# Filler products in TensorE's planned gaps among the first chunks, and GpSimd's fills behind its first weight transfers

## The chip, the cores and the metric

The kernel runs on one core of one Trainium2 chip. The metric is the device time of one execution in microseconds (us). Before the change it is 734.04 us, the median of three runs (733.62 to 735.03).

## What is computed

All is float32. A gated linear recurrence runs over 768 steps for 4 batches and 8 heads with 48 features each; its result, 3072 rows of 384 features, goes through an RMS norm and a SwiGLU feed-forward of width 1536.

```
# attention: per batch and head, state S of 48 x 48, complex gate a = a_re + i a_im
mag = sqrt(a_re^2 + a_im^2);  a = a * min(mag, 0.999) / (mag + 1e-6)
for t in range(768):
    S = a_t * S + k_t v_t^T          # complex, row-wise gate
    y_t = q_t . Re(S)
# feed-forward, over 3072 rows x of 384
xn  = x / sqrt(mean(x^2) + 1e-6) * rms_g
out = (silu(xn @ w_gate) * (xn @ w_val)) @ w_out      # 384 -> 1536 -> 384
```

The weights arrive as 64-bit words and are narrowed to float32 on the chip.

## The kernel before, in words

**Chunks, units, groups.** The sequence is cut into chunks of 128 steps: 6 per batch, 24 in all. The gates are worked out per unit (`gates`, line 990): units 0 and 1 are chunk 0 and chunk 1 alone, all others are two chunks. Two chunks make a group, and `feed` (line 1198) runs the feed-forward of a group.

**From gate to product.** For a unit, ScalarE and VectorE work out the size and the angle of the gates and the running products of both; at the end VectorE multiplies q and k with sines and cosines into a tile `rot` (lines 1057 to 1061, two products of 128x768 a chunk, about 0.95 us each). Because a head's features lie on other partitions in `rot` than TensorE needs them, six DMAs on SP's queue carry a chunk's `rot` to the tile `kq` (line 1063). With `kq` there, `attend` (line 1078) makes on TensorE: the scores `bank<-kq` (64 matmul records), masked by two `copy_predicated` into `am`; two sets of transposes `bank<-ident,kq`, copied by ScalarE to `kt`; the result `bank<-am,ve` (and `bank<-kq,state` from chunk 1 on), where `ve` is the chunk of v, loaded by DMA; and the state's increment `bank<-vn,kt`. Then the norm: ScalarE squares into `sq`, TensorE sums it with `ones`, VectorE writes `ssv`, GpSimd takes the power into `rs`, TensorE spreads it (`bank<-ident,rs`), VectorE writes `xT`. When both chunks of a group have their `xT`, the group's feed-forward runs: twelve blocks of 12 records `bank<-xT,wg` and `bank<-xT,wv` (128x256 each), then the products with `wo`.

**Weights.** `narrow` (line 906) loads twelve pieces of the weights through GpSimd's DMA queue: six of 1536 KB (gate and value parts in turns), then six of 768 KB. Three places hold raw words, so the fourth transfer must wait until VectorE has finished the first piece; `fetch` (line 885) also makes it wait for the landing of chunk 0's `kq` (`CLEAR`), and the first for the landing of the first gate load (`begun`). For each piece ScalarE converts the low words, and VectorE shifts, combines and adds: 0.95, 1.76 and 1.76 us for a large piece.

**What sets the order.** Nothing is issued as it is written. `Flow.add` (line 519) records each step with an engine, a cost, its reads and writes; `dates` (530) gives due times backwards; `schedule` (550) then plays the program through with those costs and always takes, of an engine's ready steps, the one that is due first; `issue` (645) emits in that order. So each engine has one fixed order of instructions, and a change in a cost or a due time can change the order on all engines. The planner [...]: a TensorE step gets up to 3 us more when less than 2 us of the last 4 were busy.

**Small fills.** At the start GpSimd writes constants: zeros beside the columns of `ve` and `state`, the mask `causal` (a fill and eight `affine_select`), an identity, zeros in `am` (lines 844 to 859).

Of the kernel before, what the change touches and what calls it, by code (L numbers as in the profile page):

```python
# [19 lines left out]
C = 128  # L20
# [441 lines left out]
class Flow:  # L462
# [6 lines left out]
    SYNC = 0.12  # L469
    LAND = 2.0  # L470
    LANES = 8
    BEGIN = {"SP": 0.8, "ACT": 0.8, "POOL": 0.8}
    TABLES = {"silu": ("S",), "sin": ("S", "T"), "arctan": ("T",), "rsqrt": ("A",)}

    def __init__(self, nc, rooms):
        self.nc = nc
        self.rooms = rooms
        self.ops = []
        self.seen = {}
        self.stage = None  # L480
        self.shift = {}

    def box(self, ap):
        t = ap.tensor
# [31 lines left out]
        kept.append((op["i"], write, p0, p1, lo, hi))  # L516
        self.seen[name] = kept

    def add(self, eng, calls, dur, reads=(), writes=(), table=None, land=None, due=None, after=(), behind=()):
        op = dict(i=len(self.ops), eng=eng, calls=calls, dur=dur, deps=set(), table=table, land=land,  # L520
                  base=due, stage=self.stage, behind={o["i"] for o in behind})
        self.ops.append(op)
        op["deps"].update(o["i"] for o in after)
        for ap in reads:
            self.note(op, ap, False)
        for ap in writes:
            self.note(op, ap, True)
        return op

    def dates(self):  # L530
        users = [[] for _ in self.ops]
        self.next = [[] for _ in self.ops]
        for op in self.ops:
            op["behind"] -= op["deps"]
            for d in op["deps"]:
                users[d].append(op["i"])
            for d in op["behind"]:
                self.next[d].append(op["i"])
        for op in reversed(self.ops):
            due = op["base"] if op["base"] is not None else 1e6  # L540
            for u in users[op["i"]]:
                x = self.ops[u]
                stretch = 1.0 if x["eng"] == "PE" else 1.35
                due = min(due, x["due"] - x["dur"] * stretch - (x["land"] or 0.0) - 0.2)
            op["due"] = due
        for op in self.ops:
            op["due"] += self.shift.get(op["stage"], 0.0)
        return users

    def schedule(self):  # L550
# [3 lines left out]
        free = {}  # L554
        waiting = {}
        table = None
        for op in self.ops:
            free.setdefault(op["eng"], self.BEGIN.get(op["eng"], 0.0))
            waiting.setdefault(op["eng"], [])
            if not left[op["i"]]:  # L560
                waiting[op["eng"]].append(op)
# [21 lines left out]
        while True:  # L583
            best = None
            for eng, ops in waiting.items():
                if ops:
                    t = max(free[eng], min(ready[o["i"]] for o in ops))
                    if eng == "SP" and len(sent) >= self.LANES:
                        if "landed" not in sent[-self.LANES]:
                            continue  # L590
                        t = max(t, sent[-self.LANES]["landed"])
                    if best is None or t < best[0]:
                        best = (t, eng)
            busy = [q for q in lanes.values() if q]
            if busy:
                whole = sum(q[0][1]["packet"] for q in busy)
                q = min(busy, key=lambda q: q[0][0] / q[0][1]["packet"])
                t = now + max(0.0, q[0][0]) * whole / q[0][1]["packet"]
                if best is None or t <= best[0]:
                    flows(t)  # L600
                    now = max(now, t)
                    o = q.pop(0)[1]
                    o["landed"] = now + self.LAND + (1.5 if o["eng"] == "POOL" else 0.0)
                    release(o, o["landed"])
                    continue
            if best is None:
                break
            t, eng = best
            pick = None
            for o in waiting[eng]:  # L610
                if ready[o["i"]] > t + 1e-9:
                    continue
                key = o["due"]
                if o["table"] and table not in self.TABLES[o["table"]]:
                    key += self.switch
                if pick is None or key < pick[0]:
                    pick = (key, o)
            o = pick[1]
            waiting[eng].remove(o)
            dur = o["dur"]  # L620
            if o["table"] and table not in self.TABLES[o["table"]]:
                table = self.TABLES[o["table"]][-1]
                dur += 1.3
                self.loads = getattr(self, "loads", 0) + 1
            if eng == "PE":
                busy = sum(min(e, t) - max(b, t - 4.0) for b, e in recent if e > t - 4.0)
                if busy < 2.0:
                    dur += min(dur, 3.0)
                recent.append((t, t + dur))
                del recent[:-12]  # L630
            o["start"], o["end"], o["order"] = t, t + dur, order
            order += 1
            free[eng] = t + dur
            release(o, t + dur, self.next)
            if o["land"] is not None:
                flows(t)
                now = max(now, t)
                if eng != "POOL":
                    sent.append(o)
                lanes.setdefault(eng, []).append([o["load"] + 0.05, o])  # L640
            else:
                release(o, t + dur)
        assert order == len(self.ops)

    def issue(self):
        for op in sorted(self.ops, key=lambda o: o["order"]):
            for fn, args, kw in op["calls"]:
                fn(*args, **kw)  # L648


def fast(tc, ctx, qT, kT, v, a_re, a_im, w_gate, w_val, w_out, rms_g, out, H, bad):
# [192 lines left out]
    for t, x in ((ones, 1.0), (halfpi, PI / 2), (mid, -(RE_MAX + RE_MIN) / 2),  # L844
                 (width, -(RE_MAX - RE_MIN) / 2), (mhalf, -0.5), (zeros, 0.0)):
        fill(t, x)
    for t in ves + states:
        fill(t[:, :, :, D:], 0.0)
    add("POOL", [(make_identity, (nc, ident), {})], 0.6, [], [ident])
    fill(causal, 1.0)  # L850
    for e in range(2):
        for b in range(4):
            x = causal[b * BLK:(b + 1) * BLK, e]
            add("POOL", [(nc.gpsimd.affine_select, (), dict(out=x, in_=x, pattern=[[1, C]],
                                                            compare_op=ALU.is_ge, fill=0.0,
                                                            base=-BLK * (3 - b if e else b),
                                                            channel_multiplier=-1))], 0.3, [x], [x])
    for t in ams:
        fill(t, 0.0)
    for t in banks[4:6]:  # L860
        fill(t, 0.0, eng="DVE")
    dma(gcol, rms_g.rearrange("(c p) -> p c", p=P))
# [82 lines left out]
    moved = {}  # L945
    HOLD = 1
    begun = []
    cleared = {}
    loaded = {}
    rows_ = []  # L950
# [39 lines left out]
    def gates(u):  # L990
# [66 lines left out]
        for i, n_ in enumerate(ns):  # L1057
            cs = slice(i * C, (i + 1) * C)
            for a, f in enumerate((t5, t3)):
                tt(rots[n_ % 2][:, a * ND:(a + 1) * ND].rearrange("p j (o t) -> p j o t", t=C), t["kq"][:, :, :, cs],  # L1060
                   f[:, :, cs].unsqueeze(2).to_broadcast([P, ND, 2, C]))
        for n_ in ns:
            moved[n_] = [dma(kqs[n_ % 2][r:D2:2 * ND], rots[n_ % 2][:, r], "SP") for r in range(2 * ND)]
            if n_ < 2:
                cleared[n_] = copy(seen, kqs[n_ % 2][:, 0, 0:1], eng="POOL")
# [12 lines left out]
    def attend(n):  # L1078
# [12 lines left out]
        for a in range(2):  # L1091
# [3 lines left out]
            for h in range(HH):  # L1095
                for b in range(4):
                    c = 3 - b if h % 2 else b
                    list_.append((s[c * BLK:(c + 1) * BLK, h, b * BLK:], k[:, a * HH + h, b * BLK:(b + 1) * BLK],
                                  q[:, a * HH + h, b * BLK:], True, True))
            mms(list_, HH // 2 * 0.29, due=EARLY.get(n))  # L1100
            pairs = lambda t: t.rearrange("s (m e) t -> s m e t", e=2)
            mask = causal.bitcast(I32).unsqueeze(1).to_broadcast([C, HH // 2, 2, C])
            o = am[:, a * HH:(a + 1) * HH]
# [17 lines left out]
            for x, (l_, r_) in enumerate(todo):  # L1121
                lines[c].append((o, l_, r_, x == 0, x == len(todo) - 1))
        order = [lines[c][i] for i in range(len(lines[0])) for c in range(4)]
        mms(order, len(order) * mm_time(C) / 4 * 1.1 + 0.15)
        if not last:
            kt = kts[0]
            for a in range(2):
# [6 lines left out]
            ps = banks[5][0:D2, 0:DM]  # L1134
            st = ps.rearrange("p (h d) -> p h d", h=H)
            mms([(st[c * BLK:(c + 1) * BLK, h], kt[:, h, c * BLK:(c + 1) * BLK], vv[:, h], True, True)
                 for h in range(H) for c in range(3)], H * 0.1)
            st4 = ps.rearrange("p (m e d) -> p m e d", m=NP, e=2)
            u, i = unit_of[n], n - UNITS[unit_of[n]][0]
            decay = decays[way_of(u)][:, :, i].rearrange("p (m e) -> p m e", e=2).unsqueeze(3).to_broadcast([D2, NP, 2, D])  # L1140
# [41 lines left out]
    SPREAD = 1.02  # L1182

    FIRST = 2
    B = {(k, j): wo[:, k * HD:(k + 1) * HD, j * DH:(j + 1) * DH] for k in range(2) for j in range(2)}
    blocks = lambda t: t.rearrange("p (f c) -> p f c", f=HD)
    T1 = blocks(hT[:, 4608:4608 + HD * DH])
# [110 lines left out]
    for in_, limit, op in ((ef, P_MIN, ALU.is_ge), (ef, 1.0, ALU.is_le), (range_, 0.0, ALU.is_le),  # L1298
# [11 lines left out]
                                                   scalar2=float(P * o), op0=ALU.mult, op1=ALU.add))],  # L1310
        0.2, [ps[0:1, 0:1]], [], due=clock[0] - 15.0)

    flow.schedule()
    with tc.manual_schedule():
        flow.issue()
# [50 lines left out]
```

## Time and profile before

| What | us |
|---|---|
| median of the runs shown | 734.04 |
| the profiled execution, its own time | 735.44 |
| its span, first to last instruction | 733.7 |
| TensorE busy in the span | 679.7 |
| VectorE busy | 473.2 |
| ScalarE busy | 331.3 |
| GpSimd busy | 42.0 |
| first TensorE matmul starts at | 28.22 |
| feed-forward of the first group starts at | 58.65 |

All times inside the profile are counted from the start of the span. The profiled execution spends 1.7 us outside its span. An engine's busy time is an average over the span: TensorE is nearly idle in the first tenth and nearly full afterwards, so what matters about it is read stage by stage. A matmul of float32 shows as two records, with a weight load for each.

### The profile page before, as it was taken

The numbers are of one execution on the slowest core, as the hardware profiler recorded it, in microseconds if no ns is written. First come the engines' busy times: TensorE is split into PE (matmuls) and PEld (weight loads), VectorE is DVE, ScalarE is ACT, GpSimd is POOL, SyncE is SP. The second block draws the span as 40 slices with busy tenths as digits, with TensorE's granted clock in tenths as the row PEclk, the third lists the DMA queues.
The fourth block names the chain that finished last, engine by engine and source line by source line (L and its number), as shares of the span: only waits on it lengthen the run. The fifth ranks groups of instructions, "written<-read, shape, count | busy, mean of one in ns | idle before, by whom it ended". The sixth has DMA issues, their size and how long they took to land.

```text
span 733.7 us, 16076 instructions
## 1 busy us (share of the span) xinstructions
PE 679.7 (93%) x6842; PEld 598.6 (82%) x6842; DVE 473.2 (64%) x740; ACT 331.3 (45%) x451; POOL 42.0 (6%) x80
## 2 busy tenths in 40 slices
PE   0269989999999999999999999999999999999996
PEld 0257866877888889889889889889889889889885
DVE  6979897789798887886856745765845233234121
ACT  7646856867384742841832732731830110111010
POOL 5122200000000000000000001000000000000000
PEclk9978999999999999999999999999999999999999
DMA  8597675544756625643523303313303202200000
GB/s 296 186 318 211 163 178 160 140 128 110 195 129 152 177 84 139 215 145 78 151 66 77 119 22 73 113 34 79 106 1 77 66 13 67 65 12 3 22 0 27
DMA packets 104575, 80.64 MB, mean 110 GB/s; under 512 B 42800, under 2 KB 95280, under 8 KB 104496
## 3 DMA queue, kind: packets, MB, share of 16 engines
q1 hardware_dynamic: 100432, 64.99, 33.2%
q0 software_dynamic: 3264, 14.16, 5.6%
q8 instruction: 56, 0.92, 0.5%
q10 hardware_dynamic: 800, 0.39, 0.2%
q14 instruction: 23, 0.19, 0.1%
HBM read 55.84 MB, written 4.72 MB: 83 GB/s over the span
## 4 chain that ended last, share of the span: by engine, by line
PE 64%; DVE 2%; DMA 2%; SPq 2%; ACT 1%; issue 0%; DVEq 0%; ACTq 0%
PE bank L648 64%; SPq L648 2%; DMA kq<-rot 1%; DMA in<-in_a_im_dram 1%; DVE turns L648 0%; DVE t L648 0%; ACT turns L648 0%; DVE hT L648 0%; DVE large L648 0%; DVE xT L648 0%; DVE in L648 0%; ACT L648 0%; DVE small L648 0%; DVE ot L648 0%; DVE rot L648 0%
## 5 line engine op out<-in xcount | busy, mean ns | idle before, releaser
L648 PE MATMUL bank<-xT,wg 128*128 128x256 f32 x864 | 200.8, 382 | 2.8 <-DVE xT L648 2.8
L648 PE MATMUL bank<-xT,wv 128*128 128x256 f32 x864 | 199.0, 380 | 0.0
L648 PEld LDWEIGHTS bank<-xT,wg 128*128 128x128 f32 x864 | 164.4, 191 | 25.9 <-DVE xT L648 3.5
L648 PEld LDWEIGHTS bank<-xT,wv 128*128 128x128 f32 x864 | 163.6, 190 | 22.5
L648 PE MATMUL bank<-wo,hT 128*128 128x192 f32 (+1 forms) x576 | 124.8, 360 | 0.5 <-DVE hT L648 0.4
L648 DVE TENSOR_TENSOR hT<-bank,sg 128x512 f32<-128x512 f32 x72 | 49.4, 687 | 108.6 <-PE bank L648 104.9
L648 PEld LDWEIGHTS bank<-wo,hT 128*128 128x128 f32 x576 | 94.6, 190 | 14.2 <-issue 1.4
L648 ACT ACTIVATE sg<-bank 128x512 f32<-128x512 f32 x72 | 42.8, 595 | 133.3 <-PE bank L648 132.9
L648 ACT ACT_TABLE_LOAD x68 | 87.2, 1283 | 16.3 <-DVE rot L648 8.6
L648 PE MATMUL bank<-kq 96*32 96x96 f32 (+3 forms) x1536 | 35.5, 243 | 33.8 <-DVE wg L648 28.2
L648 PEld LDWEIGHTS bank<-kq 96*32 96x32 f32 x1536 | 31.7, 114 | 39.7 <-DVE wg L648 28.2
L648 DVE TENSOR_TENSOR rot<-kin,turns 128x768 f32<-128x768 f32 x48 | 44.9, 953 | 18.4 <-DMA kq<-rot 17.5
L648 ACT ACTIVATE sq<-bank 128x384 f32<-128x384 f32 x24 | 11.7, 487 | 96.5 <-PE bank L648 95.8
L648 POOL TENSOR_TENSOR rs<-ssv,mhalf 128x1 f32<-128x1 f32 x24 | 18.4, 766 | 573.1 <-DVE ssv L648 573.1
L648 ACT ACTIVATE kt<-bank 128x384 f32<-128x384 f32 x40 | 18.4, 486 | 64.4 <-PE bank L648 63.6
L648 PE MATMUL bank<-sums,hT 128*128 128x192 f32 x240 | 45.2, 330 | 0.0
L648 PE MATMUL bank<-am,ve 128*32 128x128 f32 x768 | 41.4, 290 | 0.4 <-DMA ve<-in_v_dram 0.4
L648 PEld LDWEIGHTS bank<-sums,hT 128*128 128x128 f32 x240 | 39.4, 190 | 0.4 <-DVE mid L648 0.3
L648 DVE TENSOR_TENSOR hT<-hT 128x768 f32<-128x768 f32 x40 | 38.2, 954 | 0.9
L648 DVE COPY_PREDICATED am<-causal,bank 128x512 f32<-128x512 int32 x48 | 32.9, 720 | 8.1 <-PE bank L648 8.1
L648 ACT ACTIVATE turns<-in 128x768 f32<-128x768 f32 (+1 forms) x39 | 29.9, 789 | 14.8 <-DVE in L648 11.0
L648 PE MATMUL bank<-kq,state 96*32 96x128 f32 x640 | 35.6, 285 | 0.0
(110 smaller groups left out, 715.6 us busy)
## 6 DMA issues: line engine op xcount, KB each, us to landing
kq<-rot SPq DMA_DIRECT2D x144, 128.0 KB, 2.4
kin<-in_q_dram SPq DMA_DIRECT2D x24, 192.0 KB, 3.1
kin<-in_k_dram SPq DMA_DIRECT2D x24, 192.0 KB, 4.4
wo<-in_w_gate_dram SPq DMA_DIRECT2D x6, 768.0 KB, 4.4
out_dram<-ot SPq DMA_DIRECT2D x24, 192.0 KB, 2.2
wo<-in_w_val_dram SPq DMA_DIRECT2D x6, 768.0 KB, 5.0
wo<-in_w_out_dram SPq DMA_DIRECT2D x6, 768.0 KB, 4.7
in<-in_a_re_dram SPq DMA_DIRECT2D x11, 384.0 KB, 4.5
```

The lines of the kernel that those rows point to most:

```text
L648: fn(*args, **kw)
```

## The change

It has three parts, all within the planner and the functions that give it work.

1. **Fillers.** `schedule` notes, up to the planner's time 62, each gap on TensorE after the first product into `rot` of chunk 0, and puts so many filler products into it: the gap less 0.3, divided by 0.43. A filler is one product of 128x128 by 128x128 on data in `rot` of chunk 0, into bank 3; nothing reads the result. The planner counts the gap as busy from then on. In the program as built there are 32 fillers: 9 ahead of chunk 0's scores, 2, 6, 1 and 7 between chunk 0's steps and up to chunk 1's scores, and 1, 2 and 4 around chunk 1's norm, the last four directly ahead of the first feed-forward block.
2. **Fills.** The fills of `ve`, `state`, `causal`, the identity and `am` are given a due time of at least 12, so that GpSimd's first transfers are taken ahead of what is left of them.
3. **Costs.** The planner's costs of the scores, the results and the transitions between 32-wide and 128-wide matmuls are changed a little (`mode`; `turn` is 0, so a transition adds 0.06 to a cost and weighs nothing in the choice).

```
+        self.warm = None
+        self.fillers = []
...
+            if op["late"] is not None:
+                op["due"] = max(op["due"], op["late"])
...
+            if eng == "PE" and o["mode"] != mode:
+                mode = o["mode"]
+                dur += 0.06
+            if eng == "PE" and self.warm and t < self.warm["until"]:
+                since = max([free["PE"]] + [x["end"] + self.SYNC for x in self.warm["after"] if not recent])
+                n = int((t - since - 0.3) / 0.43)
+                if n > 0:
+                    self.fillers.append((order - 0.5, n))
+                    recent.append((since, since + 0.43 * n))
...
-        for op in sorted(self.ops, key=lambda o: o["order"]):
-            for fn, args, kw in op["calls"]:
+        steps = [(op["order"], op["calls"]) for op in self.ops]
+        steps += [(at, self.warm["call"] * n) for at, n in self.fillers]
+        for _, calls in sorted(steps, key=lambda x: x[0]):
+            for fn, args, kw in calls:
                 fn(*args, **kw)
...
+    LATE = 12.0
     for t in ves + states:
-        fill(t[:, :, :, D:], 0.0)
-    add("POOL", [(make_identity, (nc, ident), {})], 0.6, [], [ident])
-    fill(causal, 1.0)
+        fill(t[:, :, :, D:], 0.0, late=LATE)
+    add("POOL", [(make_identity, (nc, ident), {})], 0.6, [], [ident], late=LATE)
+    fill(causal, 1.0, late=LATE)
...
     for t in ams:
-        fill(t, 0.0)
+        fill(t, 0.0, late=LATE)
...
+                if not started:
+                    started.append(x)
...
-            mms(list_, HH // 2 * 0.29, due=EARLY.get(n))
+            mms(list_, HH // 2 * 0.285, due=EARLY.get(n), mode=BLK)
...
-        mms(order, len(order) * mm_time(C) / 4 * 1.1 + 0.15)
+        mms(order, len(order) * mm_time(C) / 4 * 1.06, mode=BLK)
...
-                 for h in range(H) for c in range(3)], H * 0.1)
+                 for h in range(H) for c in range(3)], H * 0.1, mode=BLK)
...
+    WARM = 62.0
...
+    filler = rots[0][:, 0]
+    flow.warm = dict(after=started, until=WARM, call=[
+        (nc.tensor.matmul, (banks[3][:, 0:C],), dict(lhsT=filler[:, 0:C], rhs=filler[:, C:2 * C], start=True, stop=True))])
```

Since the planner takes the order from its own costs, the built program also differs in the order of steps that the diff does not name, on every engine and up to the end. Around the start, these matter: on ScalarE, the conversion of the first weight piece now stands ahead of chunk 0's sines; on VectorE, the first two steps of that piece stand ahead of chunk 0's `rot`, the second step of the next piece and one `copy_predicated` of chunk 0 ahead of chunk 1's `rot`; on SP, one load of `ve` that stood ahead of chunk 1's `kq` stands behind it; on ScalarE, chunk 1's `sq` stands ahead of the work for unit 2; on TensorE, the state's increment of chunk 1 stands behind eleven blocks of the first feed-forward instead of ahead of it.

More of the change, by code (lines that the diff above doesn't have):

```diff
@@ L471 @@
     LANES = 8
+    turn = 0.0
     BEGIN = {"SP": 0.8, "ACT": 0.8, "POOL": 0.8}
@@ L517, in note, with add @@
         self.seen[name] = kept
-    def add(self, eng, calls, dur, reads=(), writes=(), table=None, land=None, due=None, after=(), behind=()):
+    def add(self, eng, calls, dur, reads=(), writes=(), table=None, land=None, due=None, after=(), behind=(), late=None, mode=None):
         op = dict(i=len(self.ops), eng=eng, calls=calls, dur=dur, deps=set(), table=table, land=land,
-                  base=due, stage=self.stage, behind={o["i"] for o in behind})
+                  base=due, late=late, mode=mode, stage=self.stage, behind={o["i"] for o in behind})
         self.ops.append(op)
@@ L556, in schedule @@
         table = None
+        mode = None
         for op in self.ops:
@@ L615, in schedule @@
                     key += self.switch
+                if eng == "PE" and o["mode"] != mode:
+                    key += self.turn
                 if pick is None or key < pick[0]:
@@ L624, in schedule @@
                 self.loads = getattr(self, "loads", 0) + 1
+            if eng == "PE" and o["mode"] != mode:
+                mode = o["mode"]
[6 more added lines that the diff above has]
+                    recent.append((since, since + 0.43 * n))
             if eng == "PE":
@@ L856, in fast @@
                                                             base=-BLK * (3 - b if e else b),
-                                                            channel_multiplier=-1))], 0.3, [x], [x])
+                                                            channel_multiplier=-1))], 0.3, [x], [x], late=LATE)
     for t in ams:
-        fill(t, 0.0)
+        fill(t, 0.0, late=LATE)
     for t in banks[4:6]:
@@ L947, in fast @@
     begun = []
+    started = []
     cleared = {}
@@ L1059, in gates @@
             for a, f in enumerate((t5, t3)):
-                tt(rots[n_ % 2][:, a * ND:(a + 1) * ND].rearrange("p j (o t) -> p j o t", t=C), t["kq"][:, :, :, cs],
+                x = tt(rots[n_ % 2][:, a * ND:(a + 1) * ND].rearrange("p j (o t) -> p j o t", t=C), t["kq"][:, :, :, cs],
                    f[:, :, cs].unsqueeze(2).to_broadcast([P, ND, 2, C]))
+                if not started:
+                    started.append(x)
         for n_ in ns:
```

## The prediction

> **What bounds the kernel now.** I read TensorE's waits first, over the whole span and then from 58 us on.
>
> ```profile
> PE bank L648 <- DVE wg L648: 28.2, 1, 28.2
> PE bank L648 <- DMA kq<-rot: 5.6, 2, 4.8
> PE bank L648 <- DVE am L648: 5.2, 2, 3.2
> ...
> PE bank L648 <- DVE xT L648: 2.8, 4, 1.0
> PE bank L648 <- DVE am L648: 2.0, 1, 2.0
> PE bank L648 <- ACT kt L648: 1.6, 1, 1.6
> PE bank L648 <- DMA kq<-rot: 0.8, 1, 0.8
> ```
>
> The last four lines are from 58 us on and, with 0.4 for hT, sum to 7.6 us in 676. So the first feed-forward block's start (58.65) and those 7.6 us decide; behind 58.65 TensorE is full. Then the timelines of TensorE, SP and GpSimd, for what sets 58.65:
>
> ```profile
> 22.04 4.16 SPq L648 DMA_DIRECT2D kq<-rot  x6
> 28.22 2.36 PE L648 MATMUL bank<-kq 96*32 96x128 f32 x64 [28.22 <-DVE wg L648]
> 30.83 0.78 POOL L648 DMA_DIRECT2D wo<-in_w_val_dram  x1 [2.19 <-DVE wg L648]
> 33.03 4.18 SPq L648 DMA_DIRECT2D kq<-rot  x6
> 43.96 2.36 PE L648 MATMUL bank<-kq 96*32 96x128 f32 x64 [4.78 <-DMA kq<-rot]
> 48.17 0.43 PE L648 MATMUL bank<-am,ve 128*32 128x128 f32 x2 [0.44 <-DMA ve<-in_v_dram]
> ...
> 58.65 4.49 PE L648 MATMUL bank<-xT,wg 128*128 128x256 f32 x12
> 62.97 2.75 PE L648 MATMUL bank<-xT,wv 128*128 128x256 f32 x12
> 98.01 1.33 PE L648 MATMUL bank<-kq 96*32 96x128 f32 x64 [0.82 <-DMA kq<-rot]
> 237.87 0.54 PE L648 MATMUL bank<-vn,kt 128*32 128x48 f32 x24 [1.65 <-ACT kt L648]
> ```
>
> Three things are to be seen. The first wait is named after VectorE's wg, but GpSimd's copy of `kq` starts at 28.20 on the landing of chunk 0's kq, and so does this matmul. The same six kq transfers took 28.20 - 22.04 = 6.2 us for chunk 0 and 43.96 - 33.03 = 10.9 us for chunk 1, when a 1536 KB weight transfer issued at 30.83 ran beside them. And the same matmuls cost 2.36 at 28 and 44, 1.33 at 98; the first feed block 62.97 - 58.65 = 4.32, the next ones 2.59. The windows by the microsecond tell why:
>
> ```profile
> 50.00:51.00 1.00, 1.00 (x28) 0.50 1.09 344
> 51.00:52.00 1.00, 1.00 (x14) 0.63 1.04 404
> ...
> 55.00:56.00 1.00, 0.00 (x0) 0.58 1.07 217
> 61.00:62.00 1.00, 1.00 (x4) 0.51 0.26 36
> 62.00:63.00 1.00, 1.00 (x7) 1.00 0.95 120
> ```
>
> (Busy, then granted clock, DMA share, GB/s.) In finer windows the clock rises at 51.8, halves at 55.2, rises at 62.0.
>
> [...] the changes are 3.4 and 6.8 us apart. The window 51.8 to 55.2 had TensorE busy 1.8 of 3.4 us (0.44 + 0.55 + 0.83) and lost the clock; 48.4 to 51.8, full, won it. [...]
>
> **The change part by part.**
>
> *Fills.* GpSimd issues the first weight transfer at 6.09, after the rest of the mask, identity and state fills: 4.73 + 0.17 (the copy it must do) gives some 4.95 in the new order, 1.1 us earlier. Four `affine_select`s (0.33 each) fall behind two issues (0.9, 0.8), done by 8.5; their reader, the first masking, comes after 29. The transfers run into the q and k loads, which are read from 13.7 on. By itself it is worth nothing: the first piece landed at 14.9 and was first touched at 19.94.
>
> *VectorE and ScalarE, chunk 0.* ScalarE's conversion of that piece (1.60) goes ahead of chunk 0's sines and the 0.60 in,mid behind: sines end at 21.05, not 20.03. VectorE fills its 1.59 us wait with the piece's first two steps (0.95 + 1.76) and the kin product it had done at 13.73, and multiplies by the sines at 21.1, not 20.06. Chunk 0's kq lands 1.0 later, 29.2.
>
> *Chunk 1's rot.* Ahead of it stand, new, 1.76 (wv) + 0.73 (one masking) + 0.55 (kin, formerly before a wait), less the 1.59 filled: its end goes from 33.88 to 35.3, its first kq issue from 33.03 to 34.45.
>
> *The collision.* The fourth weight transfer waits for VectorE's end with piece one (30.27, now 28.8) and for chunk 0's kq (29.2 + 0.44): issue 29.7, not 30.83. Relative to chunk 1's kq it is 2.5 us further ahead. Before, data flowed from 31.5, at 100 to 300 GB/s until 34 and 330 to 430 then, so some 0.5 of 1.57 MB were through when kq began (34.4). 2.5 us at 400 GB/s add 1.0: the transfer is done when kq starts. Then kq takes chunk 0's 6.2 us: 34.45 + 6.2 = 40.7, allow 41, not 43.96. The next weight transfer (37.9, not 39.11) touches its end only.
>
> *Chunk 1.* VectorE now bounds the masking: from 35.3, 0.73 + 1.75 + 0.55 + (0.95 + 1.76 + 1.76) + 0.15 + 0.95, with small gaps, is 43.9; two maskings end at 45.35, not 47.14. The result also needs the last `ve` load, which landed at 48.1; SP has four of these behind kq instead of three[...]. Bounds 45.4 and 49; I take 46.5. TensorE will have been quiet for about 3 us, so I charge the cold 3.63 (warm: 1.96 at 114.47): end 50.1, not 51.8. Then ScalarE's table load and turns (1.28 + 0.84), which held sq 1.36 us, are behind it: ssv at 52.15, not 55.00; ssv to xT stays 3.3 (1.76 of weight work between): feed at 55.5, not 58.65. The deferred state increment (1.50 cold, 0.36 of it on the path) is paid later, warm, near 0.55 to 1.2. TensorE is 2.5 ahead, VectorE 2.85.
>
> *Fillers.* 128 columns are half of a 256-column record of 216 ns, two records each: 0.22 us warm, 0.43 cold (estimates from the feed rows). Nine take 3.9 us from 23.1 on, clear of 29.2. Seven ahead of chunk 1's scores end by about 41.7 if warm and 44.3 if all of chunk 0 were cold, against a masking not due to start before 43.9: cover exists, and what it costs if not is up to 1.6 us. Because a warm filler is half the planned 0.43, they fill half of the real gaps. Around the norm, 50.1 to 55.5, I count 0.55 + 0.22 + 0.8 + 0.43 + 0.45 + 0.86 = 3.3 of 5.4 us, 61%, where 53% lost the clock and a full window won it. So the cold start of the feed (4.32 - 2.59 = 1.73) goes away with even odds: value 0.9, bounds 0 and 1.73.
>
> *After that.* At 98 TensorE waited for kq (0.8) and at 101.8 for masking (2.0): there VectorE sets the pace (27.3 of 30 us busy in 60 to 90), so TensorE's extra 0.9 is lost in those waits and VectorE's 2.85 passes on. The 1.65 at 237.87 is a state increment waiting behind ScalarE, which waited 4.67 for a gate load; in the new order it follows the twelve blocks there, so that wait goes. New stalls from the reordering can't be read; bounds 0 and 2; I keep half, 0.8. The cost edits issue nothing: transitions between tile widths were 113 in the fast program and are 120, mostly the fillers'.
>
> **Sum.** 2.85 + 0.8 = 3.65: span 733.7 to 730.05, the profiled execution from 735.44 to 731.8. It stands 1.4 above the median, which I move by the same amount: 734.04 - 3.7 = 730.3.
>
> **Rivals.**
> A (forecast), 0.52: 728.4 to 732.
> B, 0.16: the fillers hold the clock through chunk 1 and the norm and the reordering also clears the waits at 98 to 102: 1.7 for the result, 1.7 for the feed, 2 of those waits on top: 725 to 728. [...] Against: VectorE paces chunk 2.
> C, 0.18: the fillers only warm an engine that waits, since masking, `ve` and weight steps set chunk 1, and `ve` still lands at 48 or later (attend 48.5, +2.0 on A), while the late wait returns elsewhere: 732.2 to 734.4. In this case the change does not do what it says.
> D, 0.14, slower: weight steps ahead of the rotations. [...] the 10.9 us stay: 34.45 + 10.9 = 45.3, 1.4 later than now, and the `ve` loads behind it too; cold seven-filler overrun comes on top. It decides from the point where kq takes over 9.5 us (34.45 + 9.5 = 43.95); without sq's gain 735.4 to 736.5.
>
> **Chances and range.** What a measurement can tell from no change is 0.2%, 1.5 us. Faster: A, B and 0.05 of C, 0.73. Same: 0.13. Slower: D nearly whole, 0.14. The range 726.0 to 735.2 leaves out a third of B and most of D. A's own range is 728.4 to 732.
>
> **What would show it.** Right: chunk 1's scores near 41 with kq landing within 7 us of its first issue; sq directly after the result; feed at 55 to 56; no 1.6 us wait before the block near 235; PEclk at half somewhere in 44 to 55. Wrong: kq 10 us under way; `ve` named ahead of the result near 48; a first feed block still at 4.3 with feed at 58; or waits at 95 to 126 grown by what the start won.

## The result, and the profile after

| | before | changed |
|---|---|---|
| median, us | 733.83 | 727.29 |
| lowest to highest (4 runs each) | 733.16 to 735.03 | 726.68 to 729.62 |
| profiled execution | 735.44 | 729.62 |
| its span | 733.7 | 727.9 |

The ratio is 0.991, 95% interval 0.9889 to 0.9932: 6.5 us less. The profiled execution stands 2.3 us above its median for the changed kernel and 1.6 for the kernel before, so the spans show 5.8 us of this and not 6.5. All readings below are from profiled executions, and single executions of one kernel differ by some us. Sizes are therefore taken from medians, and profiles are asked for places.

TensorE's waits, over the whole span and (the last four lines) from 58 us on; the columns are us in total, times, and the longest:

```profile
PE bank L667 <- DVE rot L667: 24.8, 1, 24.8
PE bank L667 <- DMA kq<-rot: 3.6, 2, 2.6
PE bank L667 <- DVE am L667: 2.7, 2, 1.5
...
PE bank L667 <- DVE xT L667: 1.5, 3, 0.9
PE bank L667 <- DMA kq<-rot: 1.0, 1, 1.0
PE bank L667 <- issue: 0.8, 1, 0.8
PE bank L667 <- DVE hT L667: 0.4, 1, 0.4
```

The first wait ends at the first filler now, not at the scores. From 58 us on, the sum is 3.7 where it was 7.6: the 2.0 for a masking (am) and the 1.6 for kt are gone.

The timeline of TensorE (start, duration, instructions, then idle time before them):

```profile
24.80 4.21 PE L667 MATMUL bank<-rot 128*128 128x128 f32 x18 [24.80 <-DVE rot L667]
28.94 1.89 PE L667 MATMUL bank<-kq 96*32 96x128 f32 x64
...
42.71 1.42 PE L667 MATMUL bank<-kq 96*32 96x128 f32 x64 [2.56 <-DMA kq<-rot]
...
53.96 0.72 PE L667 MATMUL bank<-ident,rs 128*128 128x128 f32 x2 [1.05 <-POOL rs L667]
54.47 1.91 PE L667 MATMUL bank<-rot 128*128 128x128 f32 x8
56.18 3.40 PE L667 MATMUL bank<-xT,wg 128*128 128x256 f32 x12
59.42 2.75 PE L667 MATMUL bank<-xT,wv 128*128 128x256 f32 x12
...
94.17 1.33 PE L667 MATMUL bank<-kq 96*32 96x128 f32 x64
```

Chunk 1's scores start at 42.71 (43.96 before), the feed-forward at 56.18 (58.65), and its first block takes 59.42 - 56.18 = 3.24 (4.32). Chunk 2's scores at 94.17 wait for nothing. The last fillers were issued at 54.47 and their end is past the end of xT on VectorE (55.20 + 0.55), so they cost a few tenths.

SP's and GpSimd's timelines, for the transfers ahead of chunk 1's scores:

```profile
33.64 4.38 SPq L667 DMA_DIRECT2D kq<-rot  x6
```

```profile
29.33 0.78 POOL L667 DMA_DIRECT2D wo<-in_w_val_dram  x1
...
38.34 0.17 POOL L667 COPY junk<-wo 1x1 int32<-1x1 int32 x1 [0.23 <-DMA wo<-in_w_val_dram]
```

The weight transfer issued at 29.33 was waited for until 38.34. It was under way beside kq, and kq took 42.71 - 33.64 = 9.1 us. VectorE stood idle in the same stretch, ahead of a step of chunk 0, and the view names a kq transfer as what ended the wait:

```profile
38.69 0.55 DVE L667 TENSOR_TENSOR state<-bank,decay 96x384 f32<-96x384 f32 x1 [1.91 <-DMA kq<-rot]
```

The windows by granted clock (length, TensorE busy, clock, DMA share, GB/s); their edges are where the clock changes in this trace:

```profile
50.70:54.10 3.40, 2.02 (x16) 0.99 1.08 359
54.10:57.50 3.40, 3.40 (x14) 0.50 0.84 129
98.50:101.90 3.40, 2.38 (x79) 0.99 0.47 113
101.90:105.30 3.40, 3.40 (x7) 0.51 0.38 90
```

These rows show two windows at half clock; one stretch more, from 43.8 to 50.7, covers chunk 1's masking and its result. The first of the two begins inside the norm and takes in the feed's start, so even with the fillers the clock was lost here; it came back at 57.5, where before it came back at 62.0. The second, behind a window with 1.0 us of idle time, costs 3.4 / 2 = 1.7 us of full work.

### The profile page after: what moved, and what is told of

It is laid out like the page before. It is cut to its first block, busy times and chain, and to the rows that moved or that the text cites. A ratio compares the mean times of both kernels' runs of the same rounds, so it can differ in the third digit from the quotient of the medians.

```text
span 727.9 us, 16198 instructions
## 1 busy us (share of the span) xinstructions
PE 685.7 (94%) x6906; PEld 603.7 (83%) x6906; DVE 471.6 (65%) x740; ACT 334.1 (46%) x452; POOL 42.0 (6%) x80
## 4 chain that ended last, share of the span: by engine, by line
PE 87%; DVE 5%; DMA 3%; ACT 2%; SPq 1%; issue 1%; POOL 0%; DVEq 0%; ACTq 0%
PE bank L667 87%; DMA kq<-rot 2%; SPq L667 1%; DVE turns L667 1%; DVE rot L667 1%; DVE wg L667 1%; ACT t L667 1%; DMA in<-in_a_re_dram 1%; ACT turns L667 0%; DVE t L667 0%; DVE wo L667 0%; DVE wv L667 0%; ACT L667 0%; DVE ot L667 0%; DVE in L667 0%
## 5 line engine op out<-in xcount | busy, mean ns | idle before, releaser
L667 PE MATMUL bank<-am,ve 128*32 128x128 f32 x768 | 38.1, 281 | 0.0
L667 PE MATMUL bank<-rot 128*128 128x128 f32 x64 | 11.7, 342 | 24.8 <-DVE rot L667 24.8
```

## The experiments

In this table "second block" is the start of the second feed-forward block (56.18 + 3.24 = 59.42 for the changed kernel), "waits" is TensorE's sum from 58 us on, and "half clock" is the time lost to the granted clock from 70 to 130 us (one less the clock, summed). These three are from one profiled execution each; the ratio is from all runs (without the longest of e3_double, 737.85), against the kernel before on the same chip.

| kernel | ratio | 95% interval | second block | waits | half clock |
|---|---|---|---|---|---|
| before | 1 | | 62.97 | 7.6 | 1.7 |
| changed | 0.991 | 0.9889 to 0.9932 | 59.42 | 3.7 | 1.7 |
| a1_changed | 0.9914 | 0.9881 to 0.9947 | 58.35 | 4.4 | 0 |
| e4_no_late | 0.9915 | 0.9884 to 0.9945 | 59.53 | 4.4 | 0 |
| e9_norm_more | 0.9922 | 0.9902 to 0.9942 | 59.00 | 3.3 | 0 |
| e8_norm | 0.9932 | 0.9903 to 0.996 | 58.51 | 3.9 | 1.7 |
| e12_last_four | 0.9949 | 0.9935 to 0.9964 | 59.85 | 3.7 | 3.4 |
| e7_front | 0.9957 | 0.9938 to 0.9976 | 61.37 | 3.0 | 0 |
| e1_no_fillers | 0.9959 | 0.9946 to 0.9972 | 60.31 | 3.6 | 0 |
| e3_double | 0.9973 | 0.9952 to 0.9993 | 67.52 | 4.3 | 0 |
| e10_kq_alone | 0.9993 | 0.9971 to 1.0015 | 63.83 | 8.9 | 5.1 |
| e11_old_norm | 0.9994 | 0.9974 to 1.0014 | 62.69 | 5.9 | 1.7 |
| e2_old_order_fillers | 1.0005 | 0.999 to 1.0021 | 61.52 | 5.4 | 1.7 |
| e6_costs_only | 1.0007 | 0.9994 to 1.002 | 63.54 | 8.0 | 1.7 |

My theory after the result was that the new order of steps and the fillers each bring about half: the order by clearing the waits after 58 us, the fillers by the clock at the first block. The rivals were that the fillers do it all, in any order, and that they bring nothing.

**The order alone.** The changed kernel's order, with the fillers planned but not issued:

```
-        steps += [(at, self.warm["call"] * n) for at, n in self.fillers]
```

> The changed program's order on every engine, with the 32 fillers left out. Theory O (the new order gives the gain, the fillers' clock little): 728 to 729.5, so 4.5 to 6 us of the 6.5 stay. Theory F (the fillers' clock gives the gain): 731.5 to 733.5. In both, the first feed block should cost 4.3 us again and chunk 0's scores 2.3.

Measured: 730.25 against 733.63, 3.0 us at the ratio 0.9959, between the two expectations. The waits after 58 us are 3.6, as low as with the fillers, so it is the order that clears them. But the first block is fully cold (TensorE's timeline):

```profile
55.11 5.37 PE L666 MATMUL bank<-xT,wg 128*128 128x256 f32 x12 [1.16 <-DVE xT L666]
60.31 2.75 PE L666 MATMUL bank<-xT,wv 128*128 128x256 f32 x12
```

It takes 60.31 - 55.11 = 5.20, twice the warm 2.59 of a block. The new order is thus worth about 3 us, and the fillers the other half, 0.9959 - 0.9914 = 0.0045, 3.3 us (0.7 to 5.9 when the two intervals are taken together). The two profiles would give the order more than its 3 us: against the kernel before, the second block is 2.7 us earlier and the waits are 4.0 lower. But these two executions lie 6.3 us apart, the medians only 3.4, so about half of what they show is not typical.

How the fillers earn these 3.3 us is shown only in part. In the four profiles that have all of them in the new order (the changed kernel twice, e4 and e9) the first block is 2.0 to 2.5 us shorter than here. But the feed-forward starts 0.55 to 1.5 us later, at 55.66 to 56.57, so the second block starts only 0.8 to 2.0 us earlier, at 58.35 to 59.53 against 60.31. Behind it the profiles show no more gain: from there to the end of the span it is 667.1 us without fillers and 666.6 to 668.5 with them. The profiled execution here was 1.1 us under the median of its kernel, which may hide a part.

**The fillers alone.** The kernel before in its own order, with 30 fillers put into its gaps (12, 4, 3, 5, 1, 1, 2, 2), the planner not counting them as busy time:

```
-                    recent.append((since, since + 0.43 * n))
...
-    LATE = 12.0
+    LATE = None
...
-            mms(list_, HH // 2 * 0.285, due=EARLY.get(n), mode=BLK)
+            mms(list_, HH // 2 * 0.29, due=EARLY.get(n))
```

(and the two other costs likewise as before).

> The old program's order on every engine, with fillers (30, by the same rule) put into its planned gaps. Theory O: 732.5 to 734, at most 1.5 us gained, since the masking, the kq transfer and ScalarE still set chunk 1. Theory F: 727.5 to 730.

Measured: 733.61, ratio 1.0005. The fillers alone give nothing in the old order, though in the profiled execution the first block was warm, 61.52 - 58.82 = 2.70. TensorE's waits from 58 us on:

```profile
PE bank L666 <- DVE xT L666: 1.9, 3, 0.9
PE bank L666 <- DVE am L666: 1.5, 1, 1.5
PE bank L666 <- DMA kq<-rot: 1.2, 1, 1.2
```

The wait for a masking in chunk 2 is still there. I can't say from this profile where the block's 1.6 us went: it was the shortest of the 22 executions (731.23), and in it the sum of waits is below 7.6, not above.

**The costs alone.** The new costs of the planner and nothing else of the change:

```
-    LATE = 12.0
+    LATE = None
...
-    flow.warm = dict(after=started, until=WARM, call=[
+    unused = dict(after=started, until=WARM, call=[
```

> The old program with the new planner's costs alone: no fillers planned or issued, fills as before. Its order of instructions on TensorE is near the changed one. Theory O: 728.5 to 731, most of the gain. Theory F: 732.5 to 734.

Measured: 734.59, ratio 1.0007, where theory O had expected most of the gain. The order that pays does not come from the new costs alone. What is left is that the planner counts the gaps that it fills as busy time, which makes its own estimate of the next matmuls the warm one. This is by elimination; the counting without the new costs was not run.

**The fills.** The changed kernel with the fills' due time as before:

```
-    LATE = 12.0
+    LATE = None
```

> The changed program with the fills of the constants due as before: fillers and costs as changed, the first weight transfers issued at 6.1 us again. If the fills' part is worth nothing by itself, as forecast, within 1 us of the changed program. If the new order around the first piece of weights stands on the earlier transfer, 731 to 733.

Measured: 729.18, ratio 0.9915, beside 728.49 and 0.9914 for the changed kernel in the same comparison. The second part of the change is worth nothing that can be measured.

This run says more than that, since the due time also moves the planner's order. In its profile ScalarE and VectorE go through chunk 0 in the order of the kernel before: the first piece is converted behind the sines (19.94), chunk 1's `rot` ends at 33.9 ahead of both maskings of chunk 0, and the fourth weight transfer is issued at 30.83, all as before. It has 39 fillers instead of 32. Yet the feed starts at 56.57, against 56.18 in the changed kernel and 58.65 before. So the new order of the first 35 us isn't there without the second part of the change, and the gain doesn't need it. What this kernel shares with the changed one is further on: `sq` directly behind chunk 1's result (49.41), the state's increment behind eleven feed-forward blocks (85.53), and no masking named among the waits after 58 us.

**The changed kernel again**, without an edit, so that the next runs have it beside them:

> The changed program once more, in as many rounds as the experiments, so that they have it on the same chip beside them. Its first figure came from four runs. If the four were typical: 726.5 to 728.5. If they were lucky: 728.5 to 730.5, near the program without fillers, which then would have little left to explain.

Measured: 728.49, ratio 0.9914. Its profile is a lesson in itself. In chunk 2 it has about the same idle time as the first profile of this kernel (0.87 us before one matmul, against 1.01), but keeps the clock (length, then busy time of TensorE, its weight loads, VectorE, ScalarE and GpSimd, then clock, DMA share and GB/s; the edges are this trace's own):

```profile
96.98:100.39 3.41, 2.54 (x99) 2.34 (x92) 2.83 (x5) 2.01 (x6) 0.00 (x0) 1.00 0.49 120
100.39:103.81 3.41, 3.41 (x41) 2.01 (x41) 3.31 (x5) 1.54 (x3) 0.56 (x1) 1.00 0.32 73
```

The profiled executions were 729.62 and 727.66, 2.0 apart: 1.7 is the one window at half clock, 1.1 the earlier second block, and 0.7 goes the other way in waits. Lost clock goes with time in other runs too. For each of the 18 executions of e9_norm_more (below) the mean granted clock is on record, to 0.001 (the stretch before its first change counts as full); the span times one less the clock lies between 4.3 and 10.3 us, and the time rises by 1.2 us for each us of it (correlation 0.90). In the 22 executions without fillers the two hardly go together (0.32).

**Which fillers.** First only the 25 up to chunk 1's scores, then only the seven around its norm, and then only the last four, directly ahead of the feed-forward:

```
-        steps += [(at, self.warm["call"] * n) for at, n in self.fillers]
+        steps += [(at, self.warm["call"] * n) for at, n in self.fillers[:5]]
```

> The changed program with the 25 fillers up to chunk 1's scores, without the last seven around chunk 1's norm. Theory N (what the fillers give lies at the first feed block's cold start): 729.5 to 730.5, as without any. Theory S (it lies in chunk 0 and 1's scores and result): 727 to 728.5, as with all.

```
-        steps += [(at, self.warm["call"] * n) for at, n in self.fillers]
+        steps += [(at, self.warm["call"] * n) for at, n in self.fillers[5:]]
```

> The changed program with only the last seven fillers, around chunk 1's norm and ahead of the first feed block. Theory N: 727 to 728.5, as with all. Theory S: 729.5 to 730.5. If the two parts need each other, both this and the other half stay near 730.

```
-        steps += [(at, self.warm["call"] * n) for at, n in self.fillers]
+        steps += [(at, self.warm["call"] * n) for at, n in self.fillers[-1:]]
```

> The changed kernel with only the last four fillers, those directly ahead of the first feed-forward block. Theory 1 (the clock is held by the whole stretch from the result to the norm): [...] median 729 to 730.5, near the kernel without fillers (730.25). Theory 2 (what pays is the work right ahead of the block): block at 2.7 to 3.2 us and the time of the changed kernel, 727.3 to 728.5.

Measured: 731.25 (0.9957) with the front ones, 730.82 (0.9932) with the seven, 731.3 (0.9949) with the last four. The front ones alone bring no gain that can be measured (0.9959 without any), and the first block is cold, 61.37 - 56.16 = 5.21: in this profile the granted clock fell to half at 54.5, inside the norm, and came back at 61.3. They may even cost something. VectorE's idle time at 38.69 is 1.9 to 2.0 us in three of the four profiles with exactly these front fillers (0.67 in the fourth), and at most 0.33 in the three without them (e1, e8, e12), where chunk 1's masking starts at 42.5 to 43.1 and not at 43.5 to 44.6. Why is not shown. The seven bring the block to 58.51 - 55.62 = 2.89 and, by the middles of the intervals, some six tenths of the fillers' gain; the interval also takes in all of it, and none. The last four alone bring the block to 59.85 - 56.61 = 3.24 and yet hardly a gain in time. Their profile has two windows at half clock later on, behind a wait of 1.91 for chunk 2's kq:

```profile
98.90:102.30 3.40, 1.49 (x76) 1.00 0.31 72
102.30:105.70 3.40, 3.40 (x10) 0.50 0.10 6
105.70:109.10 3.40, 3.40 (x20) 0.50 0.52 145
```

That is 3.4 us in this one execution; whether most of its executions lose them, the profile can't tell.

**More fillers.** All doubled, and then only those in front of and inside the norm doubled and tripled:

```
-        steps += [(at, self.warm["call"] * n) for at, n in self.fillers]
+        steps += [(at, self.warm["call"] * 2 * n) for at, n in self.fillers]
```

> The changed program with each filler twice (64 products), so that a gap is filled at the warm 0.22 us as well. Theory O: within 1 us of the changed program, 726.5 to 728.5: at best the cold window at the feed's start goes, at worst the fillers overrun. Theory F: 724 to 726, since chunk 1's result (1.7 us) and the first feed block become warm.

```
-        steps += [(at, self.warm["call"] * n) for at, n in self.fillers]
+        times = (1, 1, 1, 1, 1, 2, 3, 1)
+        steps += [(at, self.warm["call"] * n * x) for (at, n), x in zip(self.fillers, times)]
```

> The changed kernel with the fillers before and in chunk 1's norm doubled and tripled (2 and 6 for 1 and 2; the last four and the front 25 stay). Theory 1 (a full window around the norm is what pays): the first feed-forward block is at 2.6 to 2.9 us in every profile where the changed kernel showed 3.24 and 2.69; about 0.2 to 0.5 us under the changed kernel, 726.8 to 728.4. Theory 2 (the added fillers stand ahead of norm matmuls and push them): block at 2.7, its start 0.5 to 1 us later, no gain, 728.5 to 730.

Doubled, 731.35 (0.9973), slower than either expectation: of the gain of 0.9914, two thirds are gone. Its timeline of TensorE shows one way:

```profile
27.73 3.77 PE L667 MATMUL bank<-rot 128*128 128x128 f32 x24
31.43 1.33 PE L667 MATMUL bank<-kq 96*32 96x128 f32 x64
...
55.34 0.43 PE L667 MATMUL bank<-am,ve 128*32 128x128 f32 x2 [8.95 <-DMA ve<-in_v_dram]
```

The fillers run past the landing of chunk 0's kq (28.89, when GpSimd's copy of it starts), and the scores start 2.5 late. A masking of chunk 0 stands ahead of chunk 1's rot on VectorE, so chunk 1's kq is issued at 34.95, not 33.64, and the `ve` loads behind it on SP at 39.32, not 38.43. In this execution they landed so late that the result waited 8.95 us; this execution (735.91) is far above the median of its kernel, so the 8.95 is not its usual price.

With 1, 2, 4 made 2, 6, 4 the block is at 59.00 - 56.30 = 2.70 without any half window behind it, and the time is 728.61 (0.9922 [0.9902, 0.9942]): no better than the changed kernel.

**The norm's fillers in the old order.** The kernel before in its own order, with the gaps noted as in the run of the fillers alone, but only the last four groups issued (1, 1, 2, 2):

```
+        steps += [(at, self.warm["call"] * n) for at, n in self.fillers[4:]]
```

> The kernel before, its order kept, with only the last four of its filler groups (1, 1, 2, 2, up to the first feed-forward block) and none ahead of the scores. Theory 1 (in the old order VectorE paces chunk 2, so a faster first block is lost in waits at 98 to 102): block 2.6 to 2.9 us instead of 4.3, TensorE's waits after 58 us grow from 7.6 by what the block wins, time within 0.2% of the kernel before (732.3 to 735). Theory 2 (the gain of the fillers does not depend on the order): 1.7 to 3.3 us faster, 730.5 to 732.

Measured: 734.74, ratio 0.9994. The time is as theory 1 said, but its reason isn't shown: these six did not keep the block warm in the profiled execution (62.69 - 58.77 = 3.92), and the waits are 5.9, not more than 7.6. So the fillers give nothing in the old order, twice measured, and why stays open.

**kq alone.** The kernel before with its fourth weight transfer held back until chunk 1's kq has landed:

```
-    CLEAR = {3: 0}
+    CLEAR = {3: 1}
```

> The kernel before with its fourth weight transfer held until chunk 1's kq has landed[...]. The forecast's figure for such a transfer: 6.2 to 6.5 us from first issue to chunk 1's scores, where before took 10.9 and the changed kernel 9.1. The rival: the small packets take 8 to 9 us here too, and the weight transfer is not what stretches them (then the ve loads or the q and k loads are). Time: scores earlier by up to 4 us, but the fourth weight piece arrives some 6 us later and VectorE's weight work with it, so 732 to 736.

Measured, on SP, TensorE and VectorE:

```profile
33.03 5.23 SPq L648 DMA_DIRECT2D kq<-rot  x6
```

```profile
40.27 1.56 PE L648 MATMUL bank<-kq 96*32 96x128 f32 x64 [1.21 <-DMA kq<-rot]
```

```profile
43.56 1.32 DVE L648 COPY_PREDICATED am<-causal,bank 128x512 f32<-128x512 int32 x2
```

Without that transfer kq takes 40.27 - 33.03 = 7.2 us, of which the six issues are 5.23; with it, 9.3 to 11.1 in the four profiles of the old order (before, e2, e6 and e11). So in the old order the six transfers took 2.1 to 3.9 us more with the weight transfer beside them. But the masking starts at 43.56, 3.3 us after the scores, since VectorE was at weight steps until then. In the changed kernel, with kq at 42.71, the masking starts at 44.56; in the profile without fillers, with kq at 40.45, it starts at 42.53, since VectorE has no idle time at 36.7 there. What a shorter kq would be worth in the changed kernel stays open. The time is 734.55 (0.9993): the weight transfer is issued at 41.66, not 30.83, and in this execution the norm waits 5.80 us behind ScalarE and the feed starts at 60.61, not 58.65.

## Why the prediction was right, and what its size missed

The direction held, and the time is within the range; the forecast of 3.7 us was too small. Its ratio would be 730.3 / 734.04 = 0.995, outside the interval measured. The 727.29 lies in B's range (725 to 728) and not in A's own (728.4 to 732), so the stated range holds because it took in B. Step by step:

- **Fills**, worth nothing: right. The first weight transfer was issued at 4.54 (forecast 4.95), and without this part the time is the same.
- **Chunk 0 and chunk 1's rot**: the way was right, the sizes too large. The scores of chunk 0 start at 28.94 (forecast 29.2), rot ends at 34.48 (35.3), the first kq issue is at 33.64 (34.45). The run with the fills as before keeps the old rot (end at 33.9) and the old kq issue (33.06) and has the same time, so the gain does not rest on these.
- **The collision**: wrong in the changed kernel's two profiles, near the forecast in others. The forecast, my estimate from the 6.2 and 10.9 us of the two kq transfers before and the GB/s beside them, was that "the transfer is done when kq starts" and that kq takes 6.2. In the first profile the transfer was done at 38.3, 4.7 us after kq's first issue, and kq took 9.1; in the second kq took 8.5. The case for slower, D, needed 9.5 and was close. But in four other profiles of the same order (e1, e8, e9 and e12) kq took 7.0 to 7.3, as little as with the transfer held back, though the transfer landed 2.5 to 4.4 us after kq's first issue in them too. What decides between 7 and 9 is not shown. Nor did VectorE simply cover the 9.1: it stood idle for 1.91 us ahead of chunk 1's masking.
- **Chunk 1 on VectorE**: right in its times, though that idle time was not among its terms. The maskings start at 44.56 and last 1.32, so end at 45.9 (forecast 45.35); ssv starts at 52.47 (52.15), xT ends at 55.75 (55.45), and ScalarE's sq stands directly behind the result at 50.40. The feed starts at 56.18 (55.5). VectorE's gain was put at 2.85 and the feed's start gained 2.47.
- **Fillers**: even odds of 1.73 for a warm first block, my estimate from two stretches of one trace (1.8 of 3.4 us busy, and full). Measured, 1.1 in the first profile (3.24), 1.6 in the second (2.69). As a value it was fair. But the new order without fillers has a colder block than before (5.20, not 4.32), so within this change the fillers shorten the block by 2.0 to 2.5 us, pay 0.55 to 1.1 of it back in these two profiles by a later start, and are worth 3.3 in the medians. The nine fillers ahead of chunk 0's scores could not begin at 23.1 as forecast: they began at 24.80, when both products into rot were done, and the scores started 0.3 us after GpSimd's copy of kq (28.62), which is what they overran.
- **The wait at 237.87** (1.65): gone, as forecast. In the changed kernel the block of that group starts at 229.72 with no wait on TensorE in the 5 us before it.
- **The waits at 98 to 102**: here the step fails that made the sum too small. It read "there VectorE sets the pace (27.3 of 30 us busy in 60 to 90), so TensorE's extra 0.9 is lost in those waits". VectorE's timeline before and after, at chunk 2's masking:

```profile
97.69 1.84 DVE L648 SCALAR_TENSOR_TENSOR wo<-hT,wo 128x768 int32<-128x768 int32 x2
...
101.07 1.32 DVE L648 COPY_PREDICATED am<-causal,bank 128x512 f32<-128x512 int32 x2
```

```profile
94.27 0.95 DVE L667 SCALAR_TENSOR_TENSOR wo<-hT,wo 128x768 int32<-128x768 int32 x1
95.14 1.36 DVE L667 COPY_PREDICATED am<-causal,bank 128x512 f32<-128x512 int32 x2
```

VectorE is as busy as before (27.3 us between 60 and 90 before, 27.95 now), but in another order: the two maskings now stand behind one such weight step, and the rest of the weight work follows them. They are 5.9 us earlier while the feed is 2.5 earlier. I had read the new order only around the start, and taken VectorE's rate for its order.
- **After that**, "I keep half, 0.8": mis-sized. The waits from 58 us on fell by 7.6 - 3.7 = 3.9, where the sum allowed 0.8 and a loss of 0.9. These are sizes of two single executions; what a typical one saves there is not shown. That low level is in every kernel with the new order (3.0 to 4.4) and in none of the others (5.4 to 8.9).

The profiled executions add up as follows: 2.5 for the feed's start, 1.1 for the first block, 3.9 for later waits, 7.5 in all. The span fell by 5.8. Of the 1.7 in between, 0.9 is the state's increment of chunk 1, which was paid at 57.22 ahead of the feed and is now paid at 85.41 behind it (0.88). Where the other 0.8 was given back is open.

Of the rivals, B came nearest in both its parts: the reordering cleared the waits at 98 to 102, and the clock was mostly better around the norm (first block 3.24 and 2.69, not 4.32). The result of chunk 1 stayed cold (46.63 to 50.27), which B had counted as warm. C is out by the time, 727.29 against its 732.2 to 734.4. Its first half does hold in the old order, where the fillers brought nothing (1.0005 and 0.9994).

## What to carry to other kernels

Where a planner makes the order, a change of its costs is a change of the whole program: read the order of every engine up to the end, since here about half of the gain came with the order alone, and the longest wait that it cleared was for a masking 40 us behind the stretch that was edited; the new order right at the start was worth nothing that could be measured. Fillers are worth what they hold until real work begins: those ahead of another quiet stretch gave nothing (0.9957, and 0.9959 without any), those around the last one seem to give most (0.9932), and doubled ones ran into the landing that they were to cover (scores 2.5 us late). A shorter first block is not a gain of the same size when the fillers also push its start (2.0 to 2.5 us shorter here, 0.55 to 1.5 later). An engine's busy share does not say that the one waiting for it can't be served sooner; its order does: VectorE was busy 27.3 us of 30 before and 27.95 after, and the masking came 5.9 us sooner.

## What the runs showed of the hardware

**One microsecond of idle time can cost 1.7 more, and the busy share of a window does not say whether it does.** In the trace of the kernel before, the granted clock changes at 41.50, 51.74, 55.16, 61.98, 102.94 and 106.36: 10.24, 3.42, 6.82, 40.96 and 3.42 us apart, within 0.1 of multiples of 3.41. A window is here a stretch of 3.4 us counted from such a change. In the changed kernel, one in which TensorE was busy 2.38 of 3.4 us was followed by one at half clock (the rows in the section on the result). But 2.39 of 3.4 kept it in the kernel without fillers:

```profile
97.70:101.10 3.40, 2.39 (x117) 1.00 0.71 190
101.10:104.50 3.40, 3.40 (x45) 1.00 0.12 6
```

Around the norm the spread is wider. The changed kernel, run again, kept the clock behind a window with 1.90 us busy (columns as for that run above):

```profile
52.61:56.03 3.41, 1.90 (x14) 1.54 (x13) 3.38 (x4) 3.40 (x7) 1.31 (x2) 1.00 1.04 220
56.03:59.44 3.41, 3.41 (x18) 3.00 (x17) 3.33 (x3) 3.38 (x4) 0.76 (x1) 1.00 0.22 36
```

The kernel with only the seven fillers around the norm, e8, lost it behind one with 2.55:

```profile
49.39:52.80 3.41, 2.55 (x28) 1.97 (x20) 0.97 (x2) 2.88 (x6) 0.74 (x1) 1.00 1.04 405
52.80:56.22 3.41, 2.90 (x12) 2.81 (x13) 3.38 (x4) 3.37 (x6) 0.71 (x2) 0.50 1.16 232
```

In the full-clock windows of all profiles up to 128 us, from the one ahead of a trace's first change of the clock on, the clock was lost behind every one with up to 1.8 us busy and kept behind every one with 2.6 or more; between these both happen (the edges are known to about 0.1 us). Windows further ahead are left out, since the profile shows 1.00 there even where matmuls are slow (2.37 us for chunk 1's scores in e12, 1.33 in e9). So in these profiles the clock was lost without an idle window (behind 2.55 us busy in e8), and no single share of busy time, as the profile counts it, is the limit. In another execution of the same kernel the windows lie elsewhere: the two profiles of the changed kernel have edges at 57.5 and 101.9 in one and at 49.2 in the other (57.5 and 49.2 are 8.3 us apart, which is no multiple of 3.4), and from 70 to 130 us one has a half window and the other none.

**A filler** of 128x128 by 128x128 in float32 took 4.21 / 9 = 0.47 us cold and 1.53 / 6 = 0.26 warm, in a row; the estimates were 0.43 and 0.22.

**The waits for the loads behind kq spread widely.** The result of chunk 1 waited for `ve` not at all, for 0.4 to 1.25, or for 8.95 us in the profiles of kernels whose four loads stood at the same place behind kq on SP.
